# Two-token pairs from chunk ten on in a gated recurrence fused with an MLP: reciprocals on ScalarE, products on VectorE, q turned by DMAs of 64 partitions

## Chip, core and metric

The kernel runs on one core of one Trainium2 chip. The metric is device microseconds of one execution. The profile is one profiled execution of the kernel before; line numbers (L...) are those of its source, if it isn't said that they are the changed kernel's.

## What is computed

A gated recurrence runs over 768 tokens for each of 4 batches and 8 heads (head size 48). Its output, seen as 3072 tokens of 384 values, goes through a two-layer MLP with a squared ReLU.

```python
for t in range(S):                                   # q, k, v, alpha: (4, 8, 768, 48), float32
    state = alpha[:, :, t, :, None] * state + np.einsum('bhd,bhe->bhde', k[:, :, t], v[:, :, t])
    y[:, :, t] = np.einsum('bhd,bhde->bhe', q[:, :, t], state)
x = y.transpose(0, 2, 1, 3).reshape(3072, 384)
r = np.maximum(x @ w_in, 0.0)                        # w_in (384, 2048), w_out (2048, 384)
out = (r * r) @ w_out
```

## The kernel before

**Chunks.** The recurrence is done in 24 chunks of 128 tokens, six to a batch. With A the running product of alpha inside a chunk, a chunk needs q·A and k/A, the masked scores of the two, the scores times v, q·A times the state that comes in, and the new state, which is (state + (k/A)ᵀv) times A at the chunk's last token. Chunks 0 to 3 are made in two double chunks with two tokens per partition (`add_super`, L634); the change leaves their steps alone. Chunks 4 to 23 go through `add_chunk` (L427), one token per partition:

- Four loads of 192 KB from SP's queue (`add_load`, L359 to L372; the DMA itself is L368): alpha, q, k, v in tiles of 128 partitions x 8 heads x 48. Each contiguous run is 48 floats, 192 bytes. The buffers hold ten chunks (`LB`, L201).
- ScalarE takes the logarithm of alpha (L438). TensorE sums it over the tokens with a triangular matrix (L448). ScalarE makes A = exp(sum) (L467) and 1/A = exp(-sum) (L471).
- Below chunk 12 (`TURN`) four narrow matmuls (L450) give the total, of which two ScalarE operations make `ae`, the decay over the chunk (L474, L477). From chunk 12 on A is written in float32 with a step of four elements (the tile `Af`, L465) and two GpSimd DMAs fetch its last row as `ae` (L484).
- VectorE makes q·A (L495; L498 where it reads `Af`) and k/A (L501) into `qk_s`. GpSimd casts v to bfloat16 (L443).
- q·A and k/A are turned (transposed): below chunk 12 (`XFROM`) by eight TensorE transposes (L508, L512) and a VectorE copy (L395), from chunk 12 on by one DMA transpose from SP's queue (L515).
- Scores on TensorE (L564), two masked products per chunk on VectorE (L570), from chunk 8 on for two chunks at once (`PAIRS`). Then the state (L595, VectorE L604, ScalarE L609) and the output y (L615, L626).
- `add_tail` (L399): ScalarE casts y (tile `xn`, L393 in a helper); it is turned by TensorE and copied, or from chunk 14 on (`XTURN`) by a DMA transpose (L414).

**MLP.** `add_moe1` (L855) multiplies by w_in, ScalarE does the ReLU (L878, 512 columns each, 96 times), VectorE squares it (L886, 96 times). `add_moe2` (L923) multiplies by w_out; ScalarE or VectorE takes the result out of PSUM (L951, L953), and GpSimd's queue writes it to memory (L961, L964; the last three tiles from SP).

**What sets the order.** Every step is an `Op` with an engine, a cost, a priority and what it depends on. `Plan.run` (L104) lists them in order of planned start, and all instructions are pinned to that order; each engine then works through its own list strictly in order, waiting on semaphores. The recurrence has priority over the MLP; `gate` (L1007) holds a chunk back by how far the MLP has come. So a product that comes late on one engine stops whatever stands behind its reader on TensorE. All matmuls are issued in one helper (L273) and all transposes in another (L276), so the profile tells them apart by tiles: `w_in_b` and `w_out_b` are the MLP, `L_s`, `qkT`, `sm`, `sb`, `qk_s`, `xn` the recurrence, `warm` is work without use that bridges the start.

Of the kernel before, what the change touches and what calls it, by code (L numbers as in the profile page):

```python
# [38 lines left out]
XB_SLACK = 2.0  # L39
# [125 lines left out]
def kernel(  # L165
# [24 lines left out]
    srcs = [(n, a.rearrange("b h (c p) d -> b c p h d", p=P)) for n, a in srcs]  # L190
# [10 lines left out]
    LB = 10  # L201
# [27 lines left out]
    )  # L229
    utri_b = consts.tile([P, 1, P], BF16)  # L230
    nc.vector.tensor_copy(utri_b[:, 0, :], utri_f)
    half_in = consts.tile([P, P], BF16)
# [21 lines left out]
    NBUF = 4  # L254
    TURN = 12
    AE_LAT = 3.6
    L_s = big.tile([P, NBUF, H, DP], BF16)
    nc.gpsimd.memset(L_s[:, :, :, D:], 0.0)
    qk_s = big.tile([P, NBUF, 2, H, DP], BF16)
    qA_s, kI_s = qk_s[:, :, 0], qk_s[:, :, 1]  # L260
    nc.gpsimd.memset(qA_s[:, :, :, D:], 0.0)
    ident_bf = consts.tile([P, P], BF16)
    make_identity(nc, ident_bf)
    nc.gpsimd.memset(kI_s[:, :, :, D:], 0.0)
    ae_s = big.tile([P, NBUF, 2, NP], FP32)
# [26 lines left out]
    LD = 1.05  # L292
# [53 lines left out]
    SRC = dict(srcs)  # L346
    EARLY = 2 * 3
    PAIRS = 8
    XFROM, XTURN = 12, 14
# [4 lines left out]
    EITHER, SLOW = {"DVE": 0.47, "POOL": 0.95}, {"POOL": 0.95}  # L354
    KI_ON = [[EITHER, EITHER], [EITHER, EITHER]]
    ST_PRIO = -12.0
    SUP = [dict() for _ in range(NS)]

    def add_load(s, nm):  # L359
        d = C[s]  # L360
        b, c = divmod(s, NCH)
        k = s // 2

        def ld():
            if s % 2 == 0:
                PAIR[k][nm] = loads.tile([P, 2, H, D], FP32, name=nm)
            d[nm] = PAIR[k][nm][:, s % 2]
            pin(nc.sync.dma_start(out=d[nm], in_=SRC[nm][b, c]))  # L368
        prev = C[s - LB]["use_" + nm] if s - LB >= 2 * NS else None
        if 0 <= k - LB // 2 < NS:  # L370
            prev = SUP[k - LB // 2]["use_" + nm]
        d["ld_" + nm] = add("DMA", LD if s < 12 else 0.95, ld, prev, lat=2.4)  # L372

    PAIR = [dict() for _ in range(NT // 2)]
# [5 lines left out]
    def add_load2(u, nm):  # L380
        d = SUP[u]
        nm, half = nm[:2], nm[2:]
        hs = slice(HH * int(half), HH * int(half) + HH) if half else slice(0, H)

        def ld():
            if nm not in d:
                d[nm] = loads.tile([P, H, 2, D], FP32, name=nm)
            pin(nc.sync.dma_start(out=d[nm][:, hs].rearrange("p h s d -> p h (s d)"), in_=SRC2[nm][0, u][:, hs]))  # L388
        d["ld_" + nm + half] = add("DMA", LD2 / 2 if half else LD2, ld, lat=2.0, at=0.8)

# [36 lines left out]
    def add_chunk(s):  # L427
        d = C[s]
        b, c = divmod(s, NCH)
        i = s % NBUF  # L430
        L, qA, kI, ae = L_s[:, i], qA_s[:, i], kI_s[:, i], ae_s[:, i].rearrange("p j n -> p n j")
        was = C[s - NBUF]
        old = was["end"] if s < 2 * NS + NBUF else None
        g = dict(prio=-10.0 + s * 0.01)
        last = c == NCH - 1
# [3 lines left out]
        ln = d["use_at"] = add("ACT", 0.41, e_ln, d["ld_at"], old or was["p0"], prio=-15.0 if s < EARLY else -5.0)  # L439

        def e_vb():
            d["vb"] = work.tile([P, H, D], BF16, name="vb", bufs=4)
            pin(nc.gpsimd.tensor_copy(d["vb"], d["vt"]))  # L443
        vb = d["use_vt"] = add("POOL", 0.55, e_vb, d["ld_vt"], old or was["end"], prio=-5.0)

        def e_p0():
            pm = d["pm"] = psum(p0, [P, 512], FP32)
            mm(pm[:, 0:HD], lhsT=utri_b[:, 0, :], rhs=L[:, :, 0:D], start=True, stop=True)  # L448
            for p in range(NP if s < TURN else 0):
                mm(pm[:, HD + p:HD + p + 1], lhsT=L[:, 2 * p:2 * p + 2, :], rhs=ones_col,  # L450
                   start=True, stop=True)
        p0 = Op("PE", 0.27 if s < TURN else 0.17, e_p0, [ln], takes=GLA_BANKS, lat=0.17, **g)
        p0.gla = s
        d["p0"] = p0

        def split(x, s):
            if s < TURN:
                return x.rearrange("p (h d) -> p h d", h=H)
            return x.rearrange("p (n j d) -> p n j d", n=NP, j=2)

        def e_A():
            if s < TURN:
                d["A"] = work.tile([P, H, D], BF16, name="A")
            else:
                d["Af"] = work.tile([P, 2, D, NP], FP32, name="Af", bufs=2)  # L465
                d["A"] = d["Af"].rearrange("p j d n -> p n j d")
            pin(nc.scalar.activation(d["A"], split(d["pm"][:, 0:HD], s), AF.Exp))  # L467

        def e_Ai():
            d["Ai"] = work.tile([P, H, D], BF16, name="Ainv")  # L470
            pin(nc.scalar.activation(d["Ai"], d["pm"][:, 0:HD].rearrange("p (h d) -> p h d", h=H), AF.Exp, scale=-1.0))  # L471

        def e_ae0():
            pin(nc.scalar.activation(ae[0:64, :, 0], d["pm"][0:64, HD:HD + NP], AF.Exp))  # L474

        def e_ae1():
            pin(nc.scalar.activation(ae[64:128, :, 1], d["pm"][64:128, HD:HD + NP], AF.Exp))  # L477
        plan.add(p0)
        a_ = add("ACT", 0.38 if s < TURN else 0.76, e_A, p0, **g)
        ai = add("ACT", 0.38, e_Ai, p0, after(a_), **g)  # L480

        def e_aed():
            for j in range(2):
                pin(nc.gpsimd.dma_start(out=ae_s[HF * j:HF * j + D, i, j], in_=d["Af"][P - 1:P, j]))  # L484
        if s < TURN:
            ae0 = add("ACT", 0.18, e_ae0, p0, after(ai), **g)
            p0.gives = ae1 = add("ACT", 0.19, e_ae1, p0, after(ae0), **g)
        else:
            p0.gives = ai
            ae1 = add("POOL", 1.03, e_aed, a_, lat=AE_LAT, prio=-20.0)  # L490
            ae1.dma = 0.42

        def e_qA():
            if s < TURN:
                pin(nc.vector.tensor_mul(qA[:, :, 0:D], d["qt"], d["A"]))  # L495
            else:
                v4 = "p (n j) d -> p n j d"
                pin(nc.vector.tensor_mul(qA[:, :, 0:D].rearrange(v4, j=2), d["qt"].rearrange(v4, j=2), d["A"]))  # L498

        def e_kI():  # L500
            pin(nc.vector.tensor_mul(kI[:, :, 0:D], d["kt"], d["Ai"]))  # L501
        mq = d["use_qt"] = add("DVE", 0.47 if s < TURN else 0.78, e_qA, a_, d["ld_qt"], old or was["cps"][0], **g)
        mk = d["use_kt"] = add("DVE", 0.47, e_kI, ai, d["ld_kt"], *([old] if old else [was["cps"][1], was.get("ps")]), **g)

        def e_p1q():
            d["pT"] = psum(p1q, [P, 2 * NP, P], BF16)
            for p in range(NP):
                tr(d["pT"][:, p, :], qA[:, 2 * p:2 * p + 2, :], ident_bf)  # L508

        def e_p1k():  # L510
            for p in range(NP):
                tr(d["pT"][:, NP + p, :], kI[:, 2 * p:2 * p + 2, :], ident_bf)  # L512
        def e_turn():
            d["qkT"] = work.tile([P, 2 * NP, P], BF16, name="qkT")
            pin(nc.sync.dma_start_transpose(out=d["qkT"], in_=qk_s[:, i].rearrange("p x h d -> p (x h d)")))  # L515
        if s < XFROM:
            p1q = plan.add(Op("PE", 0.22, e_p1q, [mq], takes=GLA_BANKS, **g))
            p1k = plan.add(Op("PE", 0.22, e_p1k, [mk, after(p1q)], lat=0.15, **g))

        def e_cp(lo, hi):  # L520
            if lo == 0:
                d["qkT"] = work.tile([P, 2 * NP, P], BF16, name="qkT")
            cast(cpk if lo else cp, d["qkT"][:, lo:hi, :], d["pT"][:, lo:hi, :])
        if s < EARLY:
            cp = add({"ACT": 0.49, "DVE": 0.34}, 0, lambda: e_cp(0, NP), p1q, **g)
            cpk = add({"DVE": 0.34, "ACT": 0.49}, 0, lambda: e_cp(NP, 2 * NP), p1k, after(cp, -9.0), **g)
        elif s < XFROM:
            cp = cpk = add("DVE", 0.61, lambda: e_cp(0, 2 * NP), p1k, was["py_op"], **g)
        else:
            cp = cpk = add("XB", 0.0, e_turn, mq, mk, was["py_op"], lat=2.8)  # L530
            cp.turn = 1.2
        if s < XFROM:
            p1q.gives = cpk

        d.update(cps=[cp, cpk], mk=mk, vb_op=vb, ae1=ae1, kI=kI, ae=ae)
        if s < PAIRS:
            add_scores(s, 1)
            add_back(s)
        elif s % 2:
            add_scores(s - 1, 2)  # L540
            add_back(s - 1)
            add_back(s)

    def add_scores(s, n):
        pr = C[s:s + n]
# [35 lines left out]
    def add_back(s):  # L581
# [45 lines left out]
        if c > 0:  # L627
            p3a = plan.add(Op("PE", 0.17, e_p3a, [cp, C[s - 1]["sb"], after(sm0)], takes=GLA_BANKS, **g))
# [439 lines left out]
```

## Time and profile before

| | us |
|---|---|
| three runs, median (lowest to highest) | 178.68 (178.56 to 180.04) |
| the profiled execution's own time | 179.8 |
| its span, first to last instruction | 178.1 |
| TensorE matmul busy | 172.0 |
| VectorE busy | 124.8 |
| ScalarE busy | 122.8 |
| GpSimd busy | 53.1 |
| DMA from SP's queue, share of 16 engines | 81.5% |

"Busy" is the time in which at least one instruction of the engine is under way. A matmul's row lasts about 0.16 us longer than its place in the stream, so a short pause of TensorE doesn't show as idle time. The chain of waits follows back what released what from the last instruction; the timeline lists instructions in order of time, with `x3` for three merged ones; the table of windows gives each engine's busy time between two moments. In groups the columns after the bar are busy time, mean duration of one, and the idle time ahead of it.

### The profile page before, as it was taken

How to read it: one execution, taken by the hardware profiler on the slowest of the kernel's cores; microseconds unless marked ns; L12 is line 12 of the kernel's file. 1: busy time of each engine (PE TensorE's matmuls, PEld its weight loads, DVE VectorE, ACT ScalarE, POOL GpSimd, SP SyncE). 2: the span in 40 equal slices, each digit the busy share in tenths (PEclk: the TensorE clock that was granted, in tenths of full speed). 3: DMA queues.
4: the chain of work that ended last, by engine and by line, in shares of the span. 5: the costliest groups of instructions: out<-in, count | busy, mean ns of one | idle time of the engine just before them, and what ended most of it. 6: DMA issues, size and time to landing. Idle time of an engine off the chain costs nothing.

```text
span 178.1 us, 4801 instructions
## 1 busy us (share of the span) xinstructions
PE 172.0 (97%) x1866; PEld 126.3 (71%) x1867; DVE 124.8 (70%) x256; ACT 122.8 (69%) x263; POOL 53.1 (30%) x95
## 2 busy tenths in 40 slices
PE   7999999999999999999999999899999999999993
PEld 3567684566896788878766786686688867757862
DVE  6699769936799798998986976798248933800600
ACT  4557789456898689979956698874598947522821
POOL 6023467711110211115222233327736080212000
PEclk9999999999999999999999999999999999999999
DMA  5999999999998999988999799999999969232012
GB/s 128 275 271 322 311 352 377 247 194 213 216 185 156 213 184 203 229 176 155 125 214 209 144 209 109 187 193 239 212 204 294 211 162 212 69 91 89 0 44 88
DMA packets 115798, 34.34 MB, mean 193 GB/s; under 512 B 109840, under 2 KB 114064, under 8 KB 115776
## 3 DMA queue, kind: packets, MB, share of 16 engines
q1 hardware_dynamic: 113536, 29.89, 81.5%
q0 software_dynamic: 2240, 4.15, 7.3%
q8 instruction: 14, 0.23, 0.6%
q14 instruction: 8, 0.07, 0.1%
HBM read 25.17 MB, written 4.72 MB: 168 GB/s over the span
## 4 chain that ended last, share of the span: by engine, by line
PE 79%; DMA 7%; DVE 4%; SPq 3%; ACT 3%; issue 1%; ACTq 0%; DVEq 0%
PE bank L273 71%; PE bank L276 4%; SPq L388 3%; DMA qt<-in_q_dram 3%; DMA at<-in_alpha_dram 3%; PE sc L273 2%; PE st L273 2%; DMA kt<-in_k_dram 2%; ACT r L878 1%; DVE sm L570 1%; ACT Af L467 1%; DVE qkT L395 1%; ACT xn L393 0%; DVE sm L763 0%; DVE xT_big L395 0%
## 5 line engine op out<-in xcount | busy, mean ns | idle before, releaser
L273 PE MATMUL bank<-xT_big,w_in_b 128*128 128x256 bf16 (+2 forms) x599 | 72.0, 268 | 0.3 <-ACT r L878 0.2
L273 PE MATMUL bank<-w_out_b,gT 128*128 128x384 bf16 (+2 forms) x400 | 69.8, 319 | 0.0
L878 ACT ACTIVATE r<-bank 128x512 bf16<-128x512 f32 x96 | 57.0, 611 | 13.5 <-PE bank L273 11.5
L886 DVE TENSOR_TENSOR gT<-r 128x512 bf16<-128x512 bf16 x96 | 46.1, 514 | 23.7 <-ACT r L878 23.4
L273 PEld LDWEIGHTS <-w_in_b 128*128 128x128 bf16 x600 | 53.2, 98 | 11.2 <-issue 1.1
L273 PEld LDWEIGHTS <-gT 128*128 128x128 bf16 x400 | 37.1, 98 | 19.4
L443 POOL CAST vb<-vt 128x384 bf16<-128x384 f32 x20 | 11.1, 553 | 58.1 <-DMA vt<-in_v_dram 30.8
L953 ACT COPY held<-bank 128x384 f32<-128x384 f32 x22 | 10.6, 481 | 14.9 <-PE bank L273 14.6
L484 POOL DMA_DIRECT2D ae_s<-Af x24 | 12.2, 511 | 25.4 <-ACT Af L467 22.2
L570 DVE TENSOR_TENSOR sm<-sc,utri_b 128x512 bf16<-128x512 f32 x24 | 15.4, 684 | 2.0 <-PE sc L273 1.8
L273 PEld LDWEIGHTS <-qkT 64*128 64x128 bf16 (+2 forms) x304 | 10.5, 97 | 5.1 <-issue 2.4
L393 ACT CAST xn<-bank 128x384 bf16<-128x384 f32 x24 | 11.1, 485 | 4.4 <-PE bank L273 4.1
L498 DVE TENSOR_TENSOR qk_s<-qt,Af 128x384 bf16<-128x384 f32 x12 | 10.2, 854 | 4.6 <-ACT Af L467 4.6
L438 ACT ACTIVATE L_s<-at 128x384 bf16<-128x384 f32 x20 | 10.6, 543 | 2.7 <-DMA at<-in_alpha_dram 2.7
L961 POOL DMA_DIRECT2D out_dram<-held x17 | 9.2, 545 | 7.9 <-ACT held L953 7.9
L467 ACT ACTIVATE Af<-bank 128x384 f32<-128x384 f32 x12 | 10.6, 883 | 0.9 <-PE bank L273 0.7
L501 DVE TENSOR_TENSOR qk_s<-kt,Ainv 128x384 bf16<-128x384 f32 x20 | 11.0, 548 | 0.0
L395 DVE COPY qkT<-bank 128x1024 bf16<-128x1024 bf16 (+1 forms) x14 | 8.3, 609 | 3.4 <-PE bank L276 3.4
L609 ACT CAST sb<-st 128x384 bf16<-128x384 f32 x16 | 8.0, 499 | 3.9 <-DVE st L604 3.8
L471 ACT ACTIVATE Ainv<-bank 128x384 bf16<-128x384 f32 x20 | 10.3, 514 | 0.0
L570 DVE TENSOR_TENSOR sm<-bank,utri_b 128x512 bf16<-128x512 f32 x16 | 10.2, 681 | 0.0
L604 DVE TENSOR_TENSOR st<-st,ae_s 128x384 f32<-128x384 f32 x16 | 8.9, 557 | 1.7 <-PE st L273 1.7
(71 smaller groups left out, 165.6 us busy)
## 6 DMA issues: line engine op xcount, KB each, us to landing
at<-in_alpha_dram SPq DMA_DIRECT2D x24, 192.0 KB, 4.0
qt<-in_q_dram SPq DMA_DIRECT2D x24, 192.0 KB, 3.8
kt<-in_k_dram SPq DMA_DIRECT2D x24, 192.0 KB, 4.0
vt<-in_v_dram SPq DMA_DIRECT2D x20, 192.0 KB, 3.9
out_dram<-held POOLq DMA_DIRECT2D x17, 192.0 KB, 4.5
wo<-in_moe_w_out_dram SPq DMA_DIRECT2D x4, 768.0 KB, 7.3
wi<-in_moe_w_in_dram SPq DMA_DIRECT2D x4, 384.0 KB, 6.8
wi<-in_moe_w_in_dram SPq DMA_DIRECT2D x2, 768.0 KB, 5.6
```

Of the source, the lines that this page charges most:

```text
L273: pin(nc.tensor.matmul(*a, **kw))
L393: pin(nc.scalar.copy(out_t, in_t))
L438: pin(nc.scalar.activation(L[:, :, 0:D], d["at"], AF.Ln))
L443: pin(nc.gpsimd.tensor_copy(d["vb"], d["vt"]))
L467: pin(nc.scalar.activation(d["A"], split(d["pm"][:, 0:HD], s), AF.Exp))
L471: pin(nc.scalar.activation(d["Ai"], d["pm"][:, 0:HD].rearrange("p (h d) -> p h d", h=H), AF.Exp, scale=-1.0))
L484: pin(nc.gpsimd.dma_start(out=ae_s[HF * j:HF * j + D, i, j], in_=d["Af"][P - 1:P, j]))
L501: pin(nc.vector.tensor_mul(kI[:, :, 0:D], d["kt"], d["Ai"]))
L570: pin(nc.vector.tensor_mul(d["sm"][:, hh], d["sc"][hh], utri_b.to_broadcast([P, NP, P])))
L878: pin(nc.scalar.activation(box["r"][:, 0:w], box["ph"][:, 0:w], AF.Relu))
L886: pin(nc.vector.tensor_mul(gT[g][:, f0:f0 + per, lo * P:lo * P + n], r, r))
L953: pin(nc.scalar.copy(box["ob"], box["po"]))
```

## The change

Chunks 4 to 9 stay as they were below chunk 12 (`add_single` in the changed kernel). Chunks 10 to 23 become seven pairs (`add_pair`). Partition p of a pair holds tokens 2p and 2p+1 of 256, so partitions 0 to 63 are one chunk and 64 to 127 the next.

- A load brings a pair, 384 KB in runs of 384 bytes. Buffers hold four pairs (`LB` 10 to 8).
- VectorE multiplies the two alphas of a partition (`pr`). The logarithm, the sum (over 64 partitions, `half_in`), A and 1/A are then done once per pair, for the second token. Eight narrow matmuls per pair give the totals, and two small ScalarE operations `ae`; the tile `Af` and GpSimd's DMAs of it are gone.
- For the first token ScalarE makes 1/alpha of the second (`l1` a logarithm, `rec` an exponential), VectorE multiplies q by it (`q0`) and k by alpha (`k0`).
- VectorE makes q·A in two products, one per token, and k/A in four products of 64 partitions, which bring the even tokens of a chunk to partitions 0 to 63 and the odd ones to 64 to 127. v is cast in four pieces of 64 partitions, two on GpSimd and two on ScalarE.
- q is turned by two DMAs of 64 partitions, k by one DMA of a pair. Turning by DMA starts at chunk 10 in place of 12, and for y at 12 in place of 14.
- The mask for these chunks (`mask_b`) is built at the start by four GpSimd casts. Tokens stay in the order even, odd; rows are written to memory in two DMAs of 64 partitions per tile, except for the last two groups of the MLP (four tiles), where the ReLU's write with a step of two elements restores the order.
- The constants of the plan are others: how far ahead a pair may start (`LEADS`), the margin ahead of a DMA transpose (`XB_SLACK` 2.0 to 1.0), priorities.

The diff, cut to its core:

```diff
-XB_SLACK = 2.0
+XB_SLACK = 1.0
-    LB = 10
+    LB = 8
...
+            nc.gpsimd.tensor_copy(mask_b[h, 0, HF * t:HF * t + HF], (sutri_f if ab > t else utri_f)[h, h])
...
-    PAIRS = 8
-    XFROM, XTURN = 12, 14
+    PAIRS = 6
+    XFROM, XTURN = 10, 12
+    LEADS = (3.5, 3.5, 4, 4, 4, 4, 4.4, 4.8, 4.95, 6.6, 6.0, 6.4)
...
+            d[nm] = loads.tile([P, H, 2, D], FP32, name=nm)
+            pin(nc.sync.dma_start(out=d[nm].rearrange("p h s d -> p h (s d)"), in_=SRC2[nm][b, c]))
...
+    def add_pair(u):
...
+            mul(op, d["pr"][:, hv[v]], d["at"][:, hv[v], 0], d["at"][:, hv[v], 1])
...
+            pin(nc.scalar.activation(L[:, hv[v], 0:D], d["pr"][:, hv[v]], AF.Ln))
...
+            pin(nc.scalar.activation(d["rec"], d["at"][:, :, 1], AF.Ln))
...
+            pin(nc.scalar.activation(d["rec"], d["rec"], AF.Exp, scale=-1.0))
...
+            mul(op, d["qt"][:, hv[v], 0], d["qt"][:, hv[v], 0], d["rec"][:, hv[v]])
...
+            mul(op, d["kt"][:, hv[v], 0], d["kt"][:, hv[v], 0], d["at"][:, hv[v], 1])
...
+            cast(op, d["vb"][o, ab], d["vt"][r, :, s])
...
+            e = {"POOL": 0.55} if s == ab else {"ACT": 0.42}
...
+            mm(pm[:, 0:W], lhsT=half_in, rhs=L[:, hv[v], 0:D], start=True, stop=True)
...
+                    mm(pm[:, HD + 2 * p:HD + 2 * p + 2], lhsT=L[:, 2 * p:2 * p + 2, :], rhs=both, start=True, stop=True)
...
+            r, o = slice(HF * ab, HF * ab + HF), slice(HF * s, HF * s + HF)
+            mul(op, dst[o, ab, :, 0:D], d[nm][r, :, s], d[f][0][r])
...
+            mul(mq[0][t], qP[:, :, t, :, 0:D], d["qt"][:, :, t].rearrange(v4, j=2), d["A"][0].rearrange(v4, j=2))
...
+                    pin(nc.sync.dma_start_transpose(out=d["qkT"][:, 1].rearrange("p t n c -> p (t n) c"),
+                                                    in_=qk_s[:, i, 1].rearrange("p t h d -> p (t h d)")))
+                else:
+                    pin(nc.sync.dma_start_transpose(out=d["qkT"][:, 0, ab].rearrange("p n (t c) -> p (n t) c", t=2),
+                                                    in_=qk_s[HF * ab:HF * ab + HF, i, 0].rearrange("p t h d -> p (t h d)")))
...
-            pin(nc.scalar.activation(d["A"], split(d["pm"][:, 0:HD], s), AF.Exp))
-                pin(nc.gpsimd.dma_start(out=ae_s[HF * j:HF * j + D, i, j], in_=d["Af"][P - 1:P, j]))
-            pin(nc.sync.dma_start_transpose(out=d["qkT"], in_=qk_s[:, i].rearrange("p x h d -> p (x h d)")))
...
-            pin(nc.scalar.activation(box["r"][:, 0:w], box["ph"][:, 0:w], AF.Relu))
+            o = box["r"][:, 0:w].rearrange("p (a c t) -> p a t c", t=2, c=HF) if g in NATURAL else box["r"][:, 0:w]
+            i = box["ph"][:, 0:w].rearrange("p (a t c) -> p a t c", t=2, c=HF) if g in NATURAL else box["ph"][:, 0:w]
+            pin(nc.scalar.activation(o, i, AF.Relu))
```

More of the change, by code (lines that the diff above doesn't have):

```diff
@@ L353, with heads @@
     SIDE = 0
-    EITHER, SLOW = {"DVE": 0.47, "POOL": 0.95}, {"POOL": 0.95}
-    KI_ON = [[EITHER, EITHER], [EITHER, EITHER]]
+    EITHER = {"DVE": 0.47, "POOL": 0.95}
     ST_PRIO = -12.0
[L357 to L374, printed above, removed]
+    NU = NT // 2
+    UB = LB // 2
+    PREP = -4.0
+    NS1 = NS + 3
+    NCU = NCH // 2
+    HEADS = 1
+    U = [dict() for _ in range(NU)]
+    SUP = U[:NS]
+    PB = 3
+    def heads(n, v):
+        return slice(H // n * v, H // n * v + H // n)
     SRC2 = [("at", alpha), ("qt", q), ("kt", k), ("vt", v)]
@@ L389, in add_load2, with add_load, ld, add_load1 @@
         d["ld_" + nm + half] = add("DMA", LD2 / 2 if half else LD2, ld, lat=2.0, at=0.8)
+    def add_load(u, nm):
+        d = U[u]
+        b, c = divmod(u, NCU)
+        def ld():
+            d[nm] = loads.tile([P, H, 2, D], FP32, name=nm)
+            pin(nc.sync.dma_start(out=d[nm].rearrange("p h s d -> p h (s d)"), in_=SRC2[nm][b, c]))
+        free = U[u - UB]["use_" + nm] if u >= UB else []
+        d["ld_" + nm] = [add("DMA", LD3, ld, *(free if isinstance(free, list) else [free]), lat=2.4)]
+    SRC1 = {n: x.rearrange("b h (c p) d -> b c p h d", p=P) for n, x in srcs}
+    def add_load1(s, nm):
+        d, u = C[s], U[s // 2]
+        b, c = divmod(s, NCH)
+        def ld():
+            if s % 2 == 0:
+                u[nm] = loads.tile([P, 2, H, D], FP32, name=nm)
+            d[nm] = u[nm][:, s % 2]
+            pin(nc.sync.dma_start(out=d[nm], in_=SRC1[nm][b, c]))
+        free = U[s // 2 - UB]["use_" + nm] if s // 2 >= UB else []
+        d["ld_" + nm] = add("DMA", LD, ld, *(free if isinstance(free, list) else [free]), lat=2.4)
+    def mul(op, out_t, a, b):
+        pin((nc.gpsimd if op.eng == "POOL" else nc.vector).tensor_mul(out_t, a, b))
+    def scaled(e, x):
+        return {k: 0.07 + (t - 0.07) * x for k, t in e.items()}
     def cast(op, out_t, in_t):
@@ new lines, in add_single @@
+    def add_single(s):
+        d, u = C[s], U[s // 2]
+        ab, i = s % 2, s // 2 % NBUF
+        early = s < EARLY
+        L, kI, qA, ae = L_s[:, s % 4], qk_s[:, i, 1, ab], qk_s[:, i, 0, ab], ae_s[:, i, ab].rearrange("p j n -> p n j")
+        was = U[s // 2 - NBUF] if s // 2 >= NBUF else None
+        wait = lambda *names: [o for x in names for o in (was[x] if was else [])]
+        g = dict(prio=-10.0 + s * 0.01)
+        if ab == 0:
+            u.update(kI=qk_s[:, i, 1], ae=ae_s[:, i].rearrange("p c j n -> p c n j"), vbs=[], mk=[], ps=[], stm=[], back=[], tq=[], tk=[], p0=[],
+                     q0=[], ln=[], cps=[], **{"use_" + nm: [] for nm, _ in srcs})
+            u["qT"] = lambda p, ab: u["qkT"][:, 0, ab, p, :]
+            u["kT"] = lambda p, ab: u["qkT"][:, 1, ab, p, :]
@@ L444, in add_chunk @@
-        vb = d["use_vt"] = add("POOL", 0.55, e_vb, d["ld_vt"], old or was["end"], prio=-5.0)
+            if ab == 0:
+                u["vb"] = work.tile([P, 2, H, D], BF16, name="vb", bufs=VB)
+            pin(nc.gpsimd.tensor_copy(u["vb"][:, ab], d["vt"]))
+        vb = add("POOL", 0.55, e_vb, d["ld_vt"], U[s // 2 - 2]["back"][ab], prio=-5.0)
+        u["use_vt"].append(vb)
+        u["vbs"] += [vb, vb]
         def e_p0():
@@ L448, in e_p0 @@
             mm(pm[:, 0:HD], lhsT=utri_b[:, 0, :], rhs=L[:, :, 0:D], start=True, stop=True)
[L449 to L452, printed above, removed]
+            for p in range(NP):
+                mm(pm[:, HD + p:HD + p + 1], lhsT=L[:, 2 * p:2 * p + 2, :], rhs=ones_col, start=True, stop=True)
@@ L493, in e_qA @@
[L493 to L514, printed above, removed]
-            pin(nc.sync.dma_start_transpose(out=d["qkT"], in_=qk_s[:, i].rearrange("p x h d -> p (x h d)")))
@@ L516, in add_chunk @@
[L516 to L542, printed above, removed]
+        plan.add(p0)
+        u["p0"].append(p0)
+        def e_exp(nm, scale):
+            d[nm] = work.tile([P, H, D], BF16, name="A" if nm == "A" else "Ainv")
+            pin(nc.scalar.activation(d[nm], d["pm"][:, 0:HD].rearrange("p (h d) -> p h d", h=H), AF.Exp, scale=scale))
@@ new lines, in add_single, with e_ae @@
+        a_ = add("ACT", 0.38, lambda: e_exp("A", 1.0), p0, **g)
+        ai = add("ACT", 0.38, lambda: e_exp("Ai", -1.0), p0, after(a_), **g)
+        def e_ae(j):
+            h = slice(HF * j, HF * j + HF)
+            pin(nc.scalar.activation(ae[h, :, j], d["pm"][h, HD:HD + NP], AF.Exp))
+        ae0 = add("ACT", 0.18, lambda: e_ae(0), p0, after(ai), *wait("stm"), **g)
+        u["ae1"] = ae1 = add("ACT", 0.19, lambda: e_ae(1), p0, after(ae0), **g)
+        p0.gives = ae1
+        mq = add("DVE", 0.47, lambda: mul(mq, qA[:, :, 0:D], d["qt"], d["A"]), a_, d["ld_qt"], *wait("tq"), **g)
@@ new lines, in add_single, with e_p1 @@
+        mk = add("DVE", 0.47, lambda: mul(mk, kI[:, :, 0:D], d["kt"], d["Ai"]), ai, d["ld_kt"], *wait("tk", "ps"), **g)
+        u["use_qt"].append(mq)
+        u["use_kt"].append(mk)
+        u["mk"].append([mk])
+        def e_p1(x):
+            if x == 0:
+                d["pT"] = psum(p1q, [P, 2, NP, P], BF16)
+            for p in range(NP):
+                tr(d["pT"][:, x, p, :], (kI if x else qA)[:, 2 * p:2 * p + 2, :], ident_bf)
+        p1q = plan.add(Op("PE", 0.22, lambda: e_p1(0), [mq], takes=GLA_BANKS, **g))
@@ new lines, in add_single, with e_cp @@
+        p1k = plan.add(Op("PE", 0.22, lambda: e_p1(1), [mk, after(p1q)], lat=0.15, **g))
+        def e_cp(x):
+            if u.get("qkT") is None:
+                u["qkT"] = work.tile([P, 2, 2, NP, P], BF16, name="qkT", bufs=QB)
+            cast(cp[x], u["qkT"][:, x, ab] if early else u["qkT"][:, :, ab], d["pT"][:, x] if early else d["pT"])
+        back2 = U[s // 2 - QB + 1]["back"] if s // 2 >= QB - 1 else []
+        cp = []
+        if early:
+            cp.append(add({"ACT": 0.49, "DVE": 0.34}, 0, lambda: e_cp(0), p1q, *back2, **g))
+            cp.append(add({"DVE": 0.34, "ACT": 0.49}, 0, lambda: e_cp(1), p1k, after(cp[0], -9.0), **g))
+        else:
+            cp.append(add("DVE", 0.61, lambda: e_cp(0), p1k, *back2, **g))
@@ L636, in add_super @@
         d = SUP[u]
-        i = 2 * u % NBUF
         pair = (C[2 * u], C[2 * u + 1])
-        L, qA, kI, ae = L_s[:, i:i + 2], qA_s[:, i:i + 2], kI_s[:, i:i + 2], ae_s[:, i:i + 2].rearrange("p b j n -> p b n j")
-        old = [C[2 * u - NBUF + ab].get("end") for ab in range(2)] if u >= 2 else []
+        L, qA, kI, ae = L_s[:, 2 * u:2 * u + 2], qk_s[:, u, 0], qk_s[:, u, 1], ae_s[:, u].rearrange("p b j n -> p b n j")
+        old = []
         g = dict(prio=-10.0 + u * 0.02)
@@ L717, in e_cp @@
         def e_cp(v):
-            d["qk"][v] = work.tile([P, 2, NH, 2, 2, HF], BF16, name="qkT")
+            if d["qk"] == [None, None]:
+                w = work.tile([P, 2, 2, NH, 2, 2, HF], BF16, name="qkT", bufs=QB)
+                d["qk"] = [w[:, 0], w[:, 1]]
             cast(cp[v], d["qk"][v], d["pT"][v])
@@ L839 @@
     NG = len(GN)
+    NATURAL = range(NG - 2, NG)
     gT = {}
```

293 lines of the change are left out of this document (208 added, 85 removed).

## The prediction

> **What bounds the kernel now.** I read the page's busy times, then the table of windows, TensorE's waits, the chain of waits, and last the timeline of VectorE.
>
> ```profile
> span 178.1 us, 4801 instructions
> ...
> PE 172.0 (97%) x1866; PEld 126.3 (71%) x1867; DVE 124.8 (70%) x256; ACT 122.8 (69%) x263; POOL 53.1 (30%) x95
> ```
>
> TensorE is busy for 97% of the span. The changed chunks lie between 62.8 us (scores of chunk 9) and 152 us (scores of the last pair):
>
> ```profile
> core 0: us, PE busy (x) PEld busy (x) DVE busy (x) ACT busy (x) POOL busy (x), PEclk, DMA share, GB/s
> 62.80:152.00 89.20, 88.66 (x952) 68.09 (x952) 68.23 (x139) 69.88 (x145) 30.11 (x57) 1.00 1.02 193
> ```
>
> There TensorE runs without a break at the full granted clock, VectorE at 76%, ScalarE at 78%, and the DMA engines are full (share 1.02). So only TensorE's own work and its few pauses can be won back. The only late arrival worth naming is one alpha load:
>
> ```profile
> 106.99 0.39 SPq L414
> 107.44 4.67 DMA at<-in_alpha_dram
> 112.13 0.03 ACT L_s L438
> 112.23 0.33 issue
> 112.56 0.59 ACT r L878
> ```
>
> The load stood behind two transposes in SP's queue; the logarithm, and a ReLU behind it, came late.
>
> ```profile
> PE bank L273 <- ACT r L878: 0.4, 2, 0.2
> PE bank L273 <- ACT L_s L438: 0.3, 1, 0.3
> ```
>
> These waits of TensorE, about 0.5 us at that place, are all that the middle has. What the change needs is VectorE time, so its rate matters:
>
> ```profile
> 71.38 0.55 DVE L604 TENSOR_TENSOR st<-st,ae_s 128x384 f32<-128x384 f32 x1
> 71.85 0.54 DVE L495 TENSOR_TENSOR qk_s<-qt,A 128x384 bf16<-128x384 f32 x1
> 72.31 0.55 DVE L501 TENSOR_TENSOR qk_s<-kt,Ainv 128x384 bf16<-128x384 f32 x1
> 72.78 1.39 DVE L886 TENSOR_TENSOR gT<-r 128x512 bf16<-128x512 bf16 x3
> 74.09 0.68 DVE L395 COPY qkT<-bank 128x1024 bf16<-128x1024 bf16 x1
> 74.69 0.78 DVE L886 TENSOR_TENSOR gT<-r 128x512 bf16<-128x512 bf16 x2
> 75.39 1.28 DVE L570 TENSOR_TENSOR sm<-sc,utri_b 128x512 bf16<-128x512 f32 x2
> ```
>
> A row lasts some 0.08 us longer than its place in the queue: from start to start a product of 384 costs 0.465 us, a masked product 0.60, a copy of q and k 0.60. A square costs 0.335 undisturbed (three last 1.08 at 87.64 us); a product from the strided tile of A costs 0.76 (starts 90.25 and 91.01).
>
> **TensorE's work.** Sixteen transposes of q and k (chunks 10, 11) and six of y (chunks 12, 13) go to DMAs: the chain has eight in 0.45 us, so 22 cost 1.22. Fourteen sums of 384 columns become seven at 0.16 (starts 103.60 and 103.76): 1.12. Eight narrow matmuls go, 28 come; eight take from 12.31 to 12.58 us, 0.034 each, so plus 0.68. Sum: 1.66 us less, all on the path. The matmuls of MLP, scores, state and output stay in number.
>
> **VectorE.** By the instruction order, between the last masked product of chunk 9 and that of chunk 23, before has 61 squares, 16 products of 384, 12 from the strided tile, 28 masked, 11 of the state, two copies of q and k, six of y, one result: 20.4 + 7.4 + 9.1 + 16.8 + 5.1 + 1.2 + 1.6 + 0.5 = 62.1 us. After has 52 squares, 61 products, 28 masked, 12 of the state, four copies, one result: 17.4 + 28.4 + 16.8 + 5.6 + 1.1 + 0.5 = 69.8. The 28 k products of 64 partitions are costed as whole ones: the row goes by elements per partition (64x64 casts last 0.19, 128x384 products 0.55). TensorE's work beside it falls by more than the change saves, since the new order puts 72 MLP matmuls of that stretch behind it (36 at 0.11, 36 at 0.16): 89.2 - 1.7 - 9.7 = 77.8 us. So VectorE goes from 68.2 to 68.2 + 7.7 = 75.9 of 77.8 us, 98%. Instructions that change partitions add to it:
>
> ```profile
> 4.13 0.18 DVE L246 CAST mask_EO<-utri_f 64x64 bf16<-64x64 f32 x1
> 4.23 0.18 DVE L247 CAST mask_EO<-utri_f 64x64 bf16<-64x64 f32 x1
> 4.42 0.19 DVE L246 CAST mask_EO<-utri_f 64x64 bf16<-64x64 f32 x1
> ```
>
> Casts follow each other in 0.10 us, but in 0.19 where they pass from partitions 0 to 63 to 64 to 127. With four such passes in each pair's k products that is 28 x 0.085 = 2.4 us: 78.3, just above 77.8. [...]
>
> What of it reaches TensorE? VectorE's 68.2 holds the tails of some 30 rows ahead of idle time, 2.4 us, which go when it no longer idles. And readers stand later than products: in the new order the first scores-times-v matmul stands some 1 us of work behind the last masked product that it needs, 2 to 5 us for chunks 16 to 19, and a DMA of k has 7 to 9 us. Bounds: 0 if this slack holds everything; 4.2 if VectorE idles 4% as at 63 to 80 us (78.3 / 0.96 = 81.6, less the 77.8, and 0.4 for the last pair's scores). I take 1.0, nearer to 0, because from 70 to 80 us VectorE is busy for 9.87 of 10 us (21 instructions) and TensorE has no wait for it there.
>
> **ScalarE.** A pair of chunks costs 2 x (0.543 + 0.883 + 0.514) = 3.88 us before. After: three logarithms or exponentials into or from float32 (0.54, 0.54, 0.51), A 0.495, 1/A 0.514, two `ae` at 0.17, two casts of v at 0.485 (the row of y's cast): 3.91. Nothing, and TensorE covers it; without cover, ScalarE at 78% has 19 us. Sixteen ReLUs write with a step of 4 bytes: 0.61 each if that is free, up to 1.09 by the row of the strided A (16-byte step, 0.883 against 0.495). I take 0.61; ScalarE is 35% busy after 154 us, so even 7.7 us more would hide except where eight follow each other over 5.1 us of matmuls: up to 3 us.
>
> **Queues.** SP issues 28 loads less (0.57 each, 16 us) and 11 transposes more; these cost at least 1.19 whatever their size (three blocks 1.19, eight 1.25): 13 us. A k turn now stands behind two of q: 2.4 us, beside the four k products (2.2). GpSimd loses 24 `ae` DMAs (12.3 us) and gains ten output DMAs (5.3), at 30% busy: nothing. Loads of the pairs have half the packets (57,344 to 28,672 of 113,536), so the DMA engines gain air; a pair's buffer comes back two chunks earlier. The late alpha load should go: minus 0.4 (0 to 0.9, the lag that TensorE gathers against its work between the scores at 99.06 and 115.64).
>
> **Start.** Four casts and larger clears on GpSimd run while VectorE builds masks; its first cast took 1.37 us beside GpSimd against 0.19 later. VectorE has 0.5 us of air before its first product at 5.46. I take 0.2 (0 to 0.6).
>
> **Sum.** -1.7 + 1.0 - 0.4 + 0.2 = -0.9 us. The profiled execution took 179.8 (178.1 and 1.7 around the span), 1.1 above the median of the three; put on the median 178.68: 177.8.
>
> **Rivals.**
> - *VectorE becomes the bound.* Place: chunks 10 to 23; it decides once products come later than their readers' 1 us. For it: 98 to 101% above. Against it: the readers' slack. With 4.2 in place of 1.0: 181.0, slower.
> - *Pauses close.* TensorE's lag behind its own work grows by some 3 us from 62.8 us to the last scores; with half the DMA packets and no strided A, 0.5 more of the pause and 1.4 of the rest go and VectorE costs 0: 174.9 at best; I give 175.9, VectorE costing 1.0.
> - *The turns come late.* Issue to landing of a turn of q and k: 3.6 to 6.6, median 4.4. A k turn behind two of q at 2.4 more than the products' 2.2, at 6.6, fills the 7 us; four pairs late by 0.65: 180.4.
> [...]
>
> **How the numbers follow.** The forecast 0.38 (176.6 to 179.2), VectorE 0.26, pauses 0.18, turns 0.09, port 0.09. About 1% (1.8 us) can be told from no change. Below 176.9: 0.16 of the pauses and 0.08 of the forecast, 0.24. Above 180.5: 0.15 of VectorE, 0.04 of the turns, 0.09 of the port, 0.28. Within: 0.48. The range 175.7 to 182.0 leaves out the ends of all cases.
>
> **What would show it.** Right: TensorE's span shrinks by some 1 us, VectorE above 93% busy over the pairs, DMA share below 0.9, `sm` and `qkT` release TensorE for about 1 us in all. Wrong: TensorE waiting some 3 us or more on `sm`, on DMA `qkT`, or on a ReLU in the last 50 us; k products that last over 0.6 us; or a first product clearly later than 5.5 us.

## The result and the profile after

The changed kernel takes 187.3 us, median of four runs (185.97 to 188.49), beside 178.79 for the kernel before on the same chip: ratio 1.046, 95% interval 1.035 to 1.056. It is slower by 8.5 us where the prediction gave 177.8 and a range up to 182.0. The profiled execution took 186.22 us, its span 184.5; it is compared below with the profiled execution of before, whose span is 178.1. The page's first lines after the change:

```profile
span 184.5 us, 4765 instructions
...
PE 172.0 (93%) x1858; PEld 125.4 (68%) x1858; DVE 136.2 (74%) x287; ACT 127.0 (69%) x280; POOL 49.7 (27%) x87
```

TensorE is busy as long as before, in a span 6.4 us longer: its busy time hides a slower clock, as the windows show. The table of windows, from the first scores of chunk 9 to the last pair's, cut at 128 us:

```profile
core 0: us, PE busy (x) PEld busy (x) DVE busy (x) ACT busy (x) POOL busy (x), PEclk, DMA share, GB/s
62.80:128.00 65.20, 62.77 (x683) 46.96 (x680) 61.34 (x127) 53.39 (x122) 11.38 (x18) 1.00 0.91 198
128.00:154.00 26.00, 22.47 (x240) 17.61 (x238) 18.94 (x41) 17.16 (x37) 11.88 (x23) 0.93 0.80 170
```

TensorE stands idle for 2.43 us of the first stretch and 3.53 of the second, at a granted clock of 0.93 there. In the kernel before the same two stretches have 0.54 and 0 at 1.00. So: 5.4 us more of pauses, 26 x 0.07 = 1.8 us of clock, less about 1 us of TensorE work saved, make 6.2 of the 6.4. The waits of TensorE from 58 to 154 us say on whom (us in total, times, longest):

```profile
PE sc L274 <- DMA qkT<-qk_s: 2.8, 1, 2.8
PE bank L274 <- ACT r L1059: 1.4, 2, 1.1
PE bank L274 <- ACT L_s L478: 1.0, 2, 0.7
PE st L274 <- ACT sb L780: 0.6, 2, 0.5
```

One wait is half of it: scores that wait for a turn of k by DMA. The chain of waits shows that turn (start, us, what): it is issued at 131.90 us and lands 7.74 us later, and the scores start with it:

```profile
131.57 0.34 issue
131.90 7.74 DMA qkT<-qk_s
139.64 0.05 issue
139.69 0.40 PE sc L274 x8
```

Why it took 7.74 us is to be read off another engine. GpSimd's timeline from 102 to 142 us (start, us, instruction, and in brackets the idle time before it and what ended it):

```profile
103.96 1.19 POOL L1146 DMA_DIRECT2D out_dram<-held  x2
123.20 1.59 POOL L423 CAST vb<-vt 64x384 bf16<-64x384 f32 x2 [18.04 <-PE bank L274]
124.73 1.03 POOL L1146 DMA_DIRECT2D out_dram<-held  x2
126.80 0.81 POOL L423 CAST vb<-vt 64x384 bf16<-64x384 f32 x1 [1.04 <-PE bank L274]
127.56 1.03 POOL L1146 DMA_DIRECT2D out_dram<-held  x2
128.64 0.91 POOL L423 CAST vb<-vt 64x384 bf16<-64x384 f32 x1
129.49 1.03 POOL L1146 DMA_DIRECT2D out_dram<-held  x2
130.52 3.22 POOL L1143 DMA_DIRECT2D out_dram<-held  x6
133.73 2.59 POOL L1146 DMA_DIRECT2D out_dram<-held  x5
```

A cast of v stands in the queue for 18 us, until TensorE gives its buffer back; the outputs behind it go out in a lump once the last casts are done. The lump falls on the turns of the last two pairs. In the kernel before, DMAs of `ae` and casts that wait stand between the outputs:

```profile
127.39 1.10 POOL L961 DMA_DIRECT2D out_dram<-held  x2
131.88 1.02 POOL L484 DMA_DIRECT2D ae_s<-Af  x2 [3.39 <-ACT Af L467]
132.89 2.16 POOL L961 DMA_DIRECT2D out_dram<-held  x4
136.15 0.51 POOL L443 CAST vb<-vt 128x384 bf16<-128x384 f32 x1 [1.10 <-DMA vt<-in_v_dram]
136.62 1.07 POOL L961 DMA_DIRECT2D out_dram<-held  x2
143.13 1.02 POOL L484 DMA_DIRECT2D ae_s<-Af  x2 [5.44 <-ACT Af L467]
144.14 2.69 POOL L961 DMA_DIRECT2D out_dram<-held  x5
```

The DMA view of 128 to 142 us in the kernel before has this:

```profile
q1 hardware_dynamic: 9113, 1.85, 77.0%
q0 software_dynamic: 640, 1.58, 33.3%
...
out_dram<-held POOLq DMA_DIRECT2D x7, 192.0 KB, 5.2
...
qkT<-qk_s SPq DMA_TRANSPOSE x2, 4.2
```

and after the change (q0 holds GpSimd's transfers: packets, MB, share of 16 engines; then KB each and median us to landing):

```profile
q0 software_dynamic: 888, 2.25, 58.5%
q1 hardware_dynamic: 3960, 0.96, 44.1%
...
out_dram<-held POOLq DMA_DIRECT2D x15, 96.0 KB, 5.0
out_dram<-held POOLq DMA_DIRECT2D x6, 192.0 KB, 4.1
qkT<-qk_s SPq DMA_TRANSPOSE x6, 6.4
```

21 outputs in place of 7 (15 of them of half the size, so 1.9 times the bytes), and six turns that share the engines with them. The engines as a whole are not fuller than before: the shares of the two queues add up to 110% before, where six loads of 192 KB stand among the rows left out, and to 103% after. So it is not the sum of the bytes that grew but what runs beside the turns; why outputs should stretch a turn more than loads do is not shown here. The fall of the clock follows the pause. TensorE by single microseconds:

```profile
139.00:140.00 1.00, 0.31 (x12) 0.32 (x14) 0.00 (x0) 0.00 (x0) 0.23 (x1) 1.00 1.11 360
140.00:141.00 1.00, 1.00 (x18) 0.78 (x13) 0.87 (x2) 0.22 (x1) 1.00 (x3) 0.84 1.07 255
141.00:142.00 1.00, 1.00 (x9) 0.73 (x8) 1.00 (x3) 0.38 (x1) 1.00 (x3) 0.50 1.21 303
142.00:143.00 1.00, 1.00 (x9) 0.73 (x7) 1.00 (x4) 0.60 (x1) 0.85 (x2) 0.50 1.86 221
143.00:144.00 1.00, 1.00 (x7) 0.67 (x6) 0.74 (x3) 0.34 (x1) 0.00 (x0) 0.50 0.47 37
```

"Busy" there is matmuls at half speed: five of 256 columns take 1.27 us from 142.08 us, nine take 1.14 us from 145.12 us.

### The profile page after: what moved, and what is told of

Same layout as the page of the kernel before. It is cut to its first block, busy times and chain, and to the rows that moved or that the text cites. A ratio compares the mean times of both kernels' runs of the same rounds, so it can differ in the third digit from the quotient of the medians.

```text
span 184.5 us, 4765 instructions
## 1 busy us (share of the span) xinstructions
PE 172.0 (93%) x1858; PEld 125.4 (68%) x1858; DVE 136.2 (74%) x287; ACT 127.0 (69%) x280; POOL 49.7 (27%) x87
## 5 line engine op out<-in xcount | busy, mean ns | idle before, releaser
L423 POOL CAST vb<-vt 64x384 bf16<-64x384 f32 x14 | 9.9, 707 | 58.4 <-PE bank L274 34.5
L1146 POOL DMA_DIRECT2D out_dram<-held x28 | 14.6, 527 | 28.6 <-ACT held L1134 25.7
L412 DVE TENSOR_TENSOR qk_s<-kt,Ainv 64x384 bf16<-64x384 f32 (+1 forms) x34 | 19.3, 568 | 0.4
L412 DVE TENSOR_TENSOR qk_s<-qt,A 128x384 bf16<-128x384 f32 x20 | 11.1, 581 | 3.6 <-ACT A L669 2.0
L738 DVE TENSOR_TENSOR sm<-sc,mask_b 128x512 bf16<-128x512 f32 x14 | 9.0, 683 | 2.1 <-PE sc L274 2.0
L274 PE MATMUL bank<-vb,sm 128*128 128x48 bf16 (+1 forms) x224 | 9.7, 182 | 0.0
L274 PEld LDWEIGHTS <-sm 128*128 128x128 bf16 (+1 forms) x224 | 8.1, 95 | 1.3 <-DVE sm L939 0.4
L738 DVE TENSOR_TENSOR sm<-bank,mask_b 128x512 bf16<-128x512 f32 x14 | 8.9, 679 | 0.0
L738 DVE TENSOR_TENSOR sm<-sc,utri_b 128x512 bf16<-128x512 f32 x12 | 7.7, 679 | 1.3 <-PE sc L274 1.3
L274 PE MATMUL sc<-qkT 64*128 64x128 bf16 (+1 forms) x136 | 6.0, 219 | 2.8 <-DMA qkT<-qk_s 2.8
(82 smaller groups left out, 178.1 us busy)
```

Source lines behind the costliest of these rows:

```text
L274: pin(nc.tensor.matmul(*a, **kw))
L412: pin((nc.gpsimd if op.eng == "POOL" else nc.vector).tensor_mul(out_t, a, b))
L423: pin(nc.gpsimd.tensor_copy(out_t, in_t))
L738: pin(nc.vector.tensor_mul(d["sm"][:, hh], d["sc"][hh], d.get("mask", mask_b).to_broadcast([P, NP, P])))
L1146: pin(q.dma_start(out=out2_r[s, t], in_=box["ob"][HF * t:HF * t + HF]))
```

## The experiments

Theory O: outputs that run beside the last turns of k are the main cost. Theory V, its rival: VectorE's products are. Runs 1 to 4 and 7 change only what single steps issue, so what is left runs in the order of the kernel that they start from. The other edits let the planner write a new order: close to the old one in 5, 9 and 10, quite another in 6, 8 and 11 to 14. Each run is given as the ratio to the kernel before on its own chip, since the medians of before differ by up to 1.5 us between chips. Every kernel's table of windows, cut as above, tells where TensorE idled:

| kernel | ratio (95% interval) | idle to 128 us | idle 128 to 154 | clock there |
|---|---|---|---|---|
| before | 1 | 0.54 | 0 | 1.00 |
| after | 1.046 (1.035 to 1.056) | 2.43 | 3.53 | 0.93 |
| 1 no products by alpha, 1/alpha | 1.040 (1.033 to 1.047) | 1.62 | 3.90 | 0.93 |
| 2 outputs of 16 tiles left out | 1.015 (1.010 to 1.020) | 2.05 | 0.81 | 1.00 |
| 3 both | 1.012 (1.008 to 1.017) | 1.78 | 0.89 | 1.00 |
| 4 k in whole products | 1.037 (1.032 to 1.042) | 0.87 | 5.35 | 0.93 |
| 5 outputs planned later | 1.052 (1.046 to 1.057) | 2.23 | 6.41 | 0.93 |
| 6 three buffers of v | 1.042 (1.035 to 1.048) | 2.25 | 3.49 | 0.93 |
| 7 before, outputs of 16 tiles left out | 0.998 (0.995 to 1.001) | 0.26 | 0 | 1.00 |
| 8 before, turning from chunk 10 | 1.004 (1.000 to 1.009) | 0.09 | 2.61 | 1.00 |
| 9 outputs behind the last turn | 1.019 (1.012 to 1.027) | 2.82 | 1.18 | 1.00 |
| 10 the same, k in whole products | 1.014 (1.006 to 1.022) | 1.42 | 1.45 | 1.00 |
| 11 as 9, products on GpSimd | 1.065 (1.055 to 1.076) | 4.83 | 4.11 | 1.00 |
| 12 as 9, three buffers of v | 1.017 (1.012 to 1.023) | - | - | - |
| 13 9, 10, 12 and 1 together | 1.011 (1.007 to 1.016) | 2.92 | 0 | 1.00 |
| 14 as 8, outputs behind the last turn | 1.021 (1.015 to 1.027) | 2.65 | 2.03 | 1.00 |

Of run 12 only the times are used.

### Products or outputs: runs 1 to 4

```
e_q0, e_k0:
-            mul(op, ...)
+            return
```


> The changed kernel without the products of q by 1/alpha and of k by alpha (q0 and k0, 14 VectorE products of 384; the first tokens' scaling is left out), in the same order otherwise. Theory V: VectorE's work is what holds the pairs back; from the scores of chunk 9 to those of pair 18/19 TensorE fell 2.9 us further behind than in the kernel before, and what follows came late because of it. 14 x 0.47 = 6.6 us less on VectorE then takes away that lag and most of the 4.0 us up to the scores of pair 20/21: 179 to 182 us. Theory O: the long pause ahead of pair 20/21 is made by output DMAs that GpSimd issues in one lump, whether VectorE is late or not: then only 2.9 us go, 184.4. If VectorE isn't the bound: within 1 us of 187.3.

```
 def e_out():
+    if s < 16:
+        return
```


> The changed kernel without the output DMAs of the first 16 tiles (their rows are not written), nothing else changed. Theory O: the k turn issued at 131.9 us took 7.7 us to land because 21 output DMAs were under way; without them it lands in about 4.4, the pause of 2.8 us and the fall of the granted clock behind it (1.3 us) go: 183 us. Theory V alone: the lag of 2.9 us up to pair 18/19 stays as it is and the pauses behind it too, 186.5 to 187.3.

Both edits together:

> Both edits at once: no q0 and k0 products, no output DMAs of the first 16 tiles. If V and O are the whole cause, the kernel comes to before less the 1.7 us of TensorE work: 177 to 178.5 us. If something else costs time (the start, the ReLU's stepped write, narrow matmuls), it stays above 180.

```
 e_mul of k:
-    r, o = slice(HF * ab, HF * ab + HF), slice(HF * s, HF * s + HF)
-    mul(op, dst[o, ab, :, 0:D], d[nm][r, :, s], d[f][0][r])
+    if ab == 0:
+        mul(op, dst[:, s, :, 0:D], d[nm][:, :, s], d[f][0])
```


> The changed kernel with the four k products of 64 partitions of each pair made as two of 128 (14 fewer; even and odd tokens are left in their partitions, so k's rows stand in another order). Theory V: 14 x 0.47 and 28 passes between partition halves at 0.085, 9.0 us less on VectorE: as e1_noscale or up to 1 us better, 178 to 181. If products of 64 partitions cost only half as much as whole ones, nothing would change: 187.

Run 1 took 186.09 us: 14 products and 6.9 us of VectorE's busy time less (129.3 in place of 136.2) bring 0.6%, which the intervals don't tell from nothing, and the pause on the turn stays (3.1 us). Theory V as a sum falls. Run 2 took 181.8: 5.5 us less than the changed kernel, no pause over 1 us, the clock at 1.00. In its DMA view of the same 14 us the turns land in 2.7 us, and the one that took 7.74 us lands in 3.2:

```profile
qkT<-qk_s SPq DMA_TRANSPOSE x6, 2.7
```

Run 3, at 181.22 us, lies 2.7 us above what was expected if V and O were the whole cause: something else stays. Run 4 tells which products do matter: with k whole, TensorE's idle time up to 128 us goes from 2.43 to 0.87, though it only removes as many instructions as run 1. The products of k stand behind 1/A, directly ahead of state and turn; those by alpha and 1/alpha can run while A isn't there yet, as at 129.89 and 130.35 us ahead of a q·A at 131.53. But the time falls by only 0.9%, which the intervals don't tell from nothing either, for two turns are now late:

```profile
PE sc L274 <- DMA qkT<-qk_s: 5.4, 2, 2.8
```

What TensorE gains ahead of a late transfer, it waits for at the transfer.

### Where the outputs lie: runs 5 to 7

```
-    OUT_AT = 118.0
+    OUT_AT = 142.0
```


> The kernel after with all outputs written, but due 24 us later in the plan (OUT_AT 142 in place of 118), so that GpSimd does all its casts of v first and no output waits behind a cast that waits for TensorE. Theory O (the lump of outputs at 124 to 142 us delays the turns of k): as without these outputs, 181.3 to 182.5 us, no pause of TensorE over 1.2 us on DMA qkT. Rival: the outputs cost by their number or bytes wherever they lie, or block the last turns at 140 to 150 us: 185 to 188. If the end is now set by outputs that land late: over 183, with a chain of waits that ends in out DMAs.

```
-    VB = 2
+    VB = 3
...
 vb waits for:
-    U[u - 2]["back"][ab]
+    U[u - 3]["back"][ab]
```


> The kernel after with three buffers for the cast values in place of two; the cast of v on GpSimd waits for the pair three back in place of two, so the queue of outputs behind it isn't held for 18 us. Outputs stay due from 118 us. Theory O: they spread over 119 to 145 us as in the kernel before, the turns of k land in 5 us or less, TensorE has no pause over 1.2 us on DMA qkT: 181.3 to 183. Rival (outputs beside turns at this place are the cost, spread or not): 185 to 188.

> Control: the kernel before without the outputs of its first 16 tiles. If the outputs are hidden there, as its trace says, it takes 178.3 to 179.2 us, no change; if the outputs cost their DMA time in any kernel, it is 3 us or more faster, and the gain of the kernel after without outputs said nothing of their place.

Both edits of the changed kernel missed, run 5 at 188.81 us and run 6 at 186.91, and their timelines of GpSimd show why. Run 5:

```profile
127.82 4.26 POOL L1146 DMA_DIRECT2D out_dram<-held  x8
132.07 3.22 POOL L1143 DMA_DIRECT2D out_dram<-held  x6
136.45 1.19 POOL L1146 DMA_DIRECT2D out_dram<-held  x2 [1.16 <-DMA out_dram<-held]
138.62 1.69 POOL L1146 DMA_DIRECT2D out_dram<-held  x3 [0.98 <-DMA out_dram<-held]
```

A due time is known to the planner only. On the chip the queue runs on as soon as its last cast is done, at 127.8 us, and the lump still falls on the turns. In run 6 no cast holds the queue for 18 us, and the lump is there all the same (16 outputs from 124.42 to 133.1 us): the late cast isn't its cause. So neither run moved the outputs off the turns, and neither could tell O from its rival. Run 7, the control, shows that the same outputs cost nothing in the kernel before: 0.998.

### Outputs behind a real wait: runs 9 to 11

```
+    mark = consts.tile([P, 8], BF16)
+    hold_out = add("POOL", 0.1, lambda: pin(nc.gpsimd.tensor_copy(mark,
+        U[NU - 1]["qkT"][:, 1, 1, NP - 1, 0:8])), *U[NU - 1]["tk"], prio=5.0)
...
 e_out:
-    ev, at=OUT_AT + 2.0 * s
+    ev, *([hold_out] if s >= 4 else []), at=OUT_AT + 2.0 * s
```


> The kernel after with all outputs written, but a copy of eight columns of the last pair's qkT stands on GpSimd ahead of the outputs of tiles 4 and up: none of them is sent before the last turn of k has landed (about 142 us). Tiles 0 to 3 stay as in the kernel after. Theory O2 (outputs that run beside the last two pairs' turns stretch these from 3 to 8 us; where they were put off by plan alone they ran beside them again): 181.3 to 182.5 us, as without these outputs, and no pause over 1.2 us on DMA qkT. Rival (these outputs cost 5 us of DMA or memory time wherever they run): 185 to 188. Over 183 with a chain of waits that ends in outputs: they come too late for the end.

> The same, and k as two products of 128 partitions for each pair in place of four of 64 (rows of k are then not in the order that the turns expect). If the two costs found so far (outputs beside turns; four half products of k on the way to state and turns, 2.4 us) are separate and all: 178.5 to 179.8 us. If the half products only mattered as a cause of late turns: as the run before, 181.3 or more.

```
 q0, k0, from pair 5:
-    "DVE", 0.47
+    "POOL", 0.95
```


> The first of these runs, and the 14 products of q and k by 1/alpha and alpha of the pairs 5 to 11 go from VectorE to GpSimd: everything is computed. Taking them out altogether, beside outputs left out, gave 0.6 us. Theory (products off the path cost little): 180.5 to 182. If GpSimd's products hold VectorE's (a shared way to the memory): over 182.5, with k products over 0.65 us.

Run 9 computes and writes everything, and its ratio, 1.019, is that of run 2 within the intervals. In us it is 183.34, 0.8 above what was expected, on a chip where the kernel before takes 180.32; in one of its four runs the clock still fell (0.991, 184.71 us). Its turns, from SP's timeline, are issued without a stretch, in 1.27 us each (in the changed kernel two half turns took 6.49 us at 133.86):

```profile
132.95 1.26 SPq L578 DMA_TRANSPOSE qkT<-qk_s  x1
134.31 2.54 SPq L581 DMA_TRANSPOSE qkT<-qk_s  x2
136.95 1.26 SPq L578 DMA_TRANSPOSE qkT<-qk_s  x1
```

Theory O is shown: not the outputs' number or bytes, but their running beside the last turns is what costs: 2.7% by this run, 3.1% by run 2. With k whole (run 10, 182.42 us) 0.6% more goes, where 1.3% was expected: the intervals overlap, and the other pauses remain. Run 11, at 191.11 us, came out 9 us above its expectation. GpSimd's products last 1.10 and 1.04 us, where VectorE's take 0.55 and 0.60 in the changed kernel, and other products of VectorE are longer than there:

```profile
L412 POOL TENSOR_TENSOR kt<-kt,at 128x384 f32<-128x384 f32 x7 | 7.7, 1095 | 4.1 <-DMA kt<-in_k_dram 3.2 <-DVE pr L412 0.5
L412 POOL TENSOR_TENSOR qt<-qt,rec 128x384 f32<-128x384 f32 x7 | 7.3, 1042 | 12.6 <-ACT rec L487 10.0 <-DMA qt<-in_q_dram 2.6
```

In its rows of VectorE `pr` lasts 922 ns (600 in the changed kernel) and k's products 638 (568): 2.3 and 2.4 us in all. The rest of the 9 us may come from q's product, which waits 10.0 us for ScalarE's reciprocals on GpSimd, with casts of v behind it, and from an order that is another; no run tells these apart.

### What stays, and the turns alone: runs 12 to 14, and 8

> Outputs of tiles 4 and up held until the last turn of k has landed, and three buffers for the cast values. With everything computed. Theory W (of the 1.9% that stay with the outputs put off, some comes from casts of v that wait on ScalarE and GpSimd for TensorE to give a buffer back, with a logarithm behind them: 1.45 us at 130.7 us in the run with whole products): ratio to before 1.005 to 1.014. Rival (VectorE's products alone make the rest): 1.017 to 1.022, no change against two buffers.

> The same with k as two whole products for each pair (rows of k not in the order that the turns expect) and without the products by alpha and 1/alpha: 28 VectorE instructions less. If VectorE's products and the buffers of v are all of the rest: ratio 0.985 to 0.998, the 1.2 to 1.7 us of TensorE work that were saved then show. If 1.005 or more: the longer way of a pair (reciprocal, product, turn) leaves pauses that a lighter VectorE doesn't close.

```
 before:
-    XFROM, XTURN = 12, 14
+    XFROM, XTURN = 10, 12
```


> Part alone, on the kernel before: q and k of chunks 10 and 11 and y of chunks 12 and 13 are turned by DMAs in place of TensorE; chunks stay single, with 128 partitions to a product. By the sum: 22 transposes less, 1.2 us less work: 177.4 to 178.0. If DMA turns of the single chunks delay TensorE wherever they are added (a rival in which the turns by DMA are the cause and not the pairing): over 179.5.

> The kernel before, q and k of chunks 10 and 11 and y of chunks 12 and 13 turned by DMAs, and the outputs of tiles 4 and up held until the turn of the last chunk has landed. Turning alone gave 1.0044, with one pause of 2.5 us on a turn of y beside outputs. If outputs beside turns make that pause: 0.990 to 0.996, faster than the kernel before. If loads or the late normalisation make it: 1.002 to 1.007. Where outputs held so long delay the end: over 1.007.

Run 12: 1.017, no change that can be told from run 9. Its interval reaches down to 1.012 and its order is another, so it only speaks against casts that wait for a buffer as the rest. Run 13, with 28 products less and VectorE busy for 50 of 65 us up to 128 (54 in the kernel before), still is at 1.011. So VectorE's load isn't the whole rest either. No single wait of its TensorE is over 0.9 us, but the longest three, 2.5 us together, are all for y on its way to the MLP, its cast and its turn:

```profile
PE bank L274 <- DMA xT_big<-xn: 0.9, 1, 0.9
PE bank L277 <- ACT xn L419: 0.9, 1, 0.9
PE bank L274 <- ACT xn L419: 0.7, 1, 0.7
```

In runs 12 and 13 the planner wrote another order, and the pauses lie elsewhere each time. What of this 1.1% belongs to the longer way of a pair (reciprocal, product, turn) and what to an order that prices it too low, these runs can't tell; it stays open.

Run 8 took 180.16 us where 177.4 to 178.0 was expected: turns by DMA save TensorE 0.8 us of busy time (171.2 beside 172.0) but don't bring it to the end even in single chunks: 1.004, with one pause, "PE bank L273 <- DMA xT_big<-xn: 2.5, 1, 2.5", on a turn of y. In run 14 that pause is gone, with the outputs held back, but three others came (ReLUs 2.3 us, a logarithm behind a late alpha load 1.3, a product of k 0.8): 1.021. None of the kernels beats the kernel before.

## Why the prediction was wrong, point by point

- **Queues: the step that failed.** "GpSimd loses 24 `ae` DMAs (12.3 us) and gains ten output DMAs (5.3), at 30% busy: nothing", and a landing of 3.6 to 6.6 us for a turn. The first counted GpSimd's time and not when its transfers would run. In the kernel before, casts and `ae` DMAs that wait for ScalarE stand between the outputs and spread them from 119.8 to 146.8 us; without them they go as fast as GpSimd issues, in some 0.52 us each (five in 2.59 us at 133.73). That the `ae` DMAs made this spacing is read from the timelines, since no run puts them back; that the overlap costs about 3% (5 us, of which 2.8 are the pause and 1.8 the clock) is shown by runs 2 and 9. The second took the landing of the kernel before (up to 6.6 us) for the new kernel's; the turn took 7.74, and 3.2 and 3.4 in runs 2 and 9. "A DMA of k has 7 to 9 us" held: the products were done at 129.2 us and TensorE came to the scores at 136.9, 7.7 us later. But the turn was issued 2.7 us after its products, behind two half turns and a turn of y in SP's queue, where the working had 2.4 less 2.2, 0.2 us; 2.7 + 7.7 = 10.4 us is 2.7 more than the slack, which is the pause.
- **The rival "turns come late"** had the right place and the wait in SP's queue, at 0.09 and 180.4. The outputs aren't in it: it priced a landing of 6.6 without a cause for more, and no fall of the clock.
- **VectorE.** 1.0 us taken, 0 to 4.2 as bounds. TensorE idles 1.9 us more up to 128 us, and run 4 takes 1.6 of that away through the products of k alone. So the size was about half of what came, within the bounds. That VectorE is at 61.34 of 65.20 us there (94%) came as forecast; that its sum decides did not (runs 1 and 13). Half products of k last 0.55 us where no cast of GpSimd runs beside them and take 0.56 to 0.59 from start to start, beside 0.465 for whole ones. The passes between the halves of the partitions were forecast, at 0.085 for each of the 28; by these starts they cost 0.09 to 0.12.
- **The late alpha load** went, as forecast: ScalarE has no wait for it in the pairs. `pr`, on VectorE behind k's products, took its place ahead of the logarithm (TensorE 1.0 us).
- **TensorE's work.** 1.66 us less was forecast, with four narrow matmuls per pair, as the trace has them (44 with `both` in place of 16), and not the eight that the section on the change gives. In run 2, at full clock, TensorE is busy for 171.1 us beside 172.0: 0.9 less, by ends that are modelled. Saved, and eaten by pauses.
- **ScalarE and the start.** ReLUs that write with a step last 0.745 us each (0.61 taken, 1.09 the bound) and no wait of TensorE follows after 154 us. Scores of chunk 9 start at 63.02 us in place of 62.75: the 0.2 of the start. (The casts compared there, 1.37 us and 0.19, are of 128x128 and of 64x64.)
- **The 0.09 for "port".** No run shows a port that GpSimd and VectorE share, or casts that hold every product. What the traces show: of the pairs' 63 products in the changed kernel, 56 last 0.54 to 0.56 us and seven 0.71 to 0.86, each beside a cast of v, and each ends some 0.41 us after that cast: at 103.56 us a q·A lasts 0.86 us, beside a cast from 103.51 to 104.02. Casts that start behind a product stretch in turn, from 0.51 to as much as 0.91 us. That is 1.6 us of VectorE's time, since few products meet a cast; what of it reaches TensorE no run separates. In the kernel before one product shows it, the q·A at 37.58 us: it lasts 0.68 us, beside a cast from 37.35 to 37.86.

## What to carry over

Before a transfer is called hidden, list what will run on the DMA engines in the same microseconds after the change, and what has spaced those transfers so far: a queue's waits are a schedule, and taking one out moves all that stands behind it. A due time in a plan doesn't hold a transfer back (run 5: the lump left at 127.8 us, due at 142); a wait does (run 9: at 142.33 us). Count an instruction by who reads its result next, not by its share in an engine's sum.

## What the runs showed of the hardware

- The granted clock fell to 0.50 for 3.41 us after a pause of TensorE of 2.79 us (136.90 to 139.69 us), and in runs 1, 4, 5 and 6 after 2.78 to 3.49 us; it did not after 2.50 us in run 8, 2.58 in run 4 (to 136.19 us) or 2.83 in run 11. So a pause of 2.8 us may cost 1.7 us more, and needn't. In the changed kernel the clock rises at 4.14 us, falls at 140.68 and rises at 144.09, which are 40 steps of 3.413 us and one; in the kernel before it stays at 1.00 from 7.09 us for 170.67, 50 such steps. TensorE was idle for 2.42 us of the step just ahead of the fall, and in no other step of these two traces, up to their last matmul, for more than 1.15; the pause of 2.58 us in run 4, counted back in such steps from its fall at 144.92, lies across a border, 1.5 us and 1.1. That the place of a pause divides the cases is the author's estimate from these numbers: no run moves a pause to test it.
- A turn of 64 partitions occupied SP's queue as long as one of 128 (in run 9, from 132.95 us on, 1.26 us for one of 128 and 2.54 for two of 64), so halving one doubles its issue. In the changed kernel the medians are 1.27 us for 64 and 1.77 for 128, and beside the outputs a half turn's issue stretched to 3.2 us.
